# Window attention and SwiGLU on one core: block 0's down projections ahead of the third block's gates, and two groups of transposes moved from the matrix engine to the DMA crossbar

## The chip, the cores and the metric

The kernel runs on one core of a Trainium2 chip. The core has a matrix engine (PE, with its weight loads shown as PEld), a vector engine (DVE), an activation engine (ACT), a general engine (POOL) and a sync engine (SP). Each takes its instructions in order and waits at semaphores. SP, ACT and POOL also issue DMA transfers, which 16 DMA engines carry out. The metric is device time in microseconds (us) from launch to end, as the median over runs.

## The reference

Two stages. First attention with a window of 128 positions and 4 sink positions (the first four keys, which every query sees), for 4 batches, 8 heads, 768 positions, head size 64. Then a SwiGLU layer over the 3072 tokens, width 512, hidden width 1536.

```python
def _attn_ref(q, k, v, n_sink, window):
    scores = scale * np.matmul(q, k.transpose(0, 1, 3, 2))
    keep = is_sink | in_window                     # pos < 4, or 0 <= rel < 128
    scores = np.where(keep, scores, -1000000000.0)
    a = np.exp(scores - np.max(scores, axis=-1, keepdims=True))
    a = a / (np.sum(a, axis=-1, keepdims=True) + 1e-09)
    return np.matmul(a, v).astype(np.float32)

def _moe_ref(x, w_gate, w_val, w_out):
    g = x @ w_gate
    silu = g * (1.0 / (1.0 + np.exp(-g)))
    return (silu * (x @ w_val) @ w_out).astype(np.float32)
```

The output of the attention, heads side by side, is x of the second stage.

## The kernel before

**Groups and blocks.** The attention runs over 12 groups of 256 queries (three per batch), the second stage over blocks of tokens: 256, 256, 256, 512, 512, 512, 512, 256. Blocks 0 and 1 (groups 0 and 1) share their gate matmuls ("01"), the third block, number 2, is group 2, and block 3 is groups 3 and 4.

**A group's steps.** load_nat fetches keys (i = 0) and queries (i = 1) of a group by POOL's DMA queue into a tile nat, in two halves of 128 rows each. They have to be turned so that the head dimension lies on partitions (tiles kT and qT). Either step_TN does it on PE (four 128x128 transposes for a half, tile pn, with an eviction by ACT or DVE, L283 or L285), or xbar does it by DMA transposes that SP issues (L293). step_S, or step_S1 to S3 from group 3 on, are the scores and their exponentials; step_K is the sinks' part (matmuls mm_K with kss, which step_ks fills, and an exponential). step_PV multiplies with the values and normalises into xn, on DVE, or on ACT where its last argument is "a". step_X turns xn into the second stage's operand xT: for groups in PEX on PE (tile px, L543, evicted at L546 or L550), for the others by a DMA transpose of SP (L538).

**Second stage.** A unit gate makes hidden slices: project with w_gate into pg (L564), a tanh on ACT (L584), project with w_val into pv, and two DVE operations (L592, and L598, L603 or L607) that write the slice into ht. A unit down makes 128 rows of output: 12 matmuls over ht and w_out (pd, L657), a copy to ot (L662), and an output DMA that ACT issues for blocks 0 to 2 and SP for the others (L665).

**Order.** Everything is written out by hand. A list us holds units (gates and downs), and weave runs them in turn; slots gives each unit, by its number, the attention steps that are put inside it. In the first weave the units 0 to 3 are the first gates of blocks 0 and 1, 4 to 11 their shared gates, 12 to 17 block 2's gates, 18 to 23 the downs of blocks 0, 1 and 2, two units each. Inside a gate the steps stand between the pg and the pv matmuls (a step marked ahead stands before pg), inside a down they are spread over its 12 matmuls. The DMA transposes of step_X, and some DVE work, are put into a list later, which flush empties at the end of a unit.

**Queues.** SP's DMA queue holds, in this order, early loads, eight small sink loads for group 0's batch, eight for the other batches (load_sinks into vcl, L211), and then the crossbar transposes. Each DMA of SP and ACT takes one of eight completion lanes (semaphores) in turn, and waits until the lane's previous DMA has landed. The sink loads into vcl wait for a POOL memset (L815) that stands behind load_nat(3) and load_v(3). POOL's queue holds the weights and the groups' inputs: gates, nat of group 2, values, w_out in four parts (load_out, L169), nat and values of group 3, then those of group 4 and so on. From group 4 on there is one nat buffer, so load_nat(5) waits for the transposes of group 4.

Of the kernel before, what the change touches and what calls it, by code (L numbers as in the profile page):

```python
# [14 lines left out]
def kernel(  # L15
# [26 lines left out]
    SIZES = [256, 256, 256, 512, 512, 512, 512, 256]  # L42
    assert sum(SIZES) == NTOK and NG == 12
    OFF = [sum(SIZES[:i]) for i in range(len(SIZES))]
    PEX = (0, 1, 2)
    QG = [g for g in range(4, NG) if g % GC]
    ONE = range(3, NG)

# [57 lines left out]
    def load_nat(g):  # L106
        b, c = divmod(g, GC)
        x = (natp if g > 3 else rowp).tile(
            [P, 2, 2, DM], BF16, tag="nat" if g > 3 else "rows", name="nat")
        for i, src in ((0, k), (1, q)):  # L110
            for j in range(2):
                t0 = c * 256 + j * P
                nc.gpsimd.dma_start(  # L113
                    x[:, i, j].rearrange("p (h d) -> p h d", d=D),
                    src[b, :, t0:t0 + P].rearrange("h p d -> p h d"))
        nats[g] = x
# [67 lines left out]
    one = const.tile([P, 1], FP32)  # L184
# [338 lines left out]
    def step_X(g, j, evict="v"):  # L523
# [6 lines left out]
        elif tb > 1 and off == 0:  # L530
            xTs[tb] = dense(xtp.tile([P, DMC * 512], BF16, tag="xT", name="xT"),
                            DMC, SIZES[tb])
            if tb == 3:
                for i in range(2):
                    xTs[tb, i] = xTs[tb][:, :, 256 * i:256 * (i + 1)]
        if g not in PEX:
            def sp():
                nc.sync.dma_start_transpose(xTs[tb][:, :, off:off + P], xns[g, j])  # L538
# [128 lines left out]
    def gates(tb):  # L667
        return [(gate, tb, f) for f in range(0, DFC, 512 // SIZES[tb])]

    def downs(tb):  # L670
        return [(down, tb, t) for t in range(SIZES[tb] // P)]

    def A(fn, *a):
        return lambda: fn(*a)

    def TN(g, evict="av"):
        return [A(step_TN, g, i, j, evict) for j in range(2) for i in range(2)]
# [4 lines left out]
    def S1(g, apart=False):  # L682
        f = A(step_S1, g, apart)
        f.ahead = True
        return f

    def one(at, g, apart=False):
        return [(at, [S1(g, apart), A(step_S2, g, apart)]), (at + 1, [A(step_S3, g)])]

    def ahead(f):  # L690
        g = lambda: f()
        g.ahead = True
        return g

    def PVs(g):
        return [A(step_PV, g, j, hh) for hh in range(2) for j in range(2)]

    def Xs(g):
        return [A(step_X, g, j) for j in range(2)]
# [104 lines left out]
    load_gate(2)  # L804
    step_vsb(0)
    load_nat(2)
    load_gate(3)
    load_v(2)
    load_gate(4)
    load_gate(5)  # L810
    for i in range(4):
        load_out(i)
    load_nat(3)
    load_v(3)
    nc.gpsimd.memset(vcl, 0.0)  # L815
# [27 lines left out]
    for f in masks1[:3]:  # L843
        f()

    g0, g1, g2 = gates(0), gates(1), gates(2)
    us = [(gate_held, *g0[0][1:]), (gate_first, *g0[1][1:]), g1[0], g1[1],
          *((gate, "01", f) for f in range(4, DFC)),
          *g2, *downs(0), *downs(1), *downs(2)]

    def L(*fs):
        def f():
            for x in fs:
                x()
        return f

    def NV(g):
        return L(A(load_nat, g), A(load_v, g))
# [1 line left out]
    weave(us, slots(  # L860
        (4, TN(2)[::2]), (5, TN(2)[1::2]), ((6, 7), Ss(2)), (6, [K(2)]),
        ((8, 8), PVs(2)[:2]), (9, [A(step_PV, 2, 0, 1, "a"), A(step_PV, 2, 1, 1, "a")]),
        ((10, 11), [A(step_X, 2, 0, "a"), ahead(A(step_X, 2, 1, "a"))]),
        (11, [NV(4), lambda: nc.gpsimd.tensor_copy(out=vcl[64:128], in_=vcl[0:64])]),
        ((14, 14, 15, 15), TN(3, "aa")),
        (15, [A(xbar, 4)]), (15, [A(load_nat, 5)]), (19, [A(xbar, 5, (0,))]),
        *one(17, 3), (18, [A(step_ks, 1)]), (18, [A(step_vsb, 1)]),
        ((19, 19, 19, 20), PVs(3)), (19, [S1(4)]), (20, [L(A(step_S2, 4), A(step_S3, 4))]), (20, Xs(3)), (20, [A(xbar, 5, (1,))]),
        ((21, 21, 21, 22), PVs(4)), (21, Xs(4)[:1]),
        (22, [Xs(4)[1], flush, A(behind, 3, 511), A(load_v, 5), A(load_nat, 6)]),  # L870
        (23, [A(xbar, 6), A(turned, 6), A(load_v, 6), NV(7)])))
# [53 lines left out]
```

## Time and profile before

Three runs: 233.52 us median, 232.6 to 233.66.

| What | Value |
|---|---|
| profiled execution, its own time | 233.03 us |
| its span, first to last instruction | 231.2 us |
| DVE, ACT, POOL busy | 151.1, 106.3, 84.8 us |
| pg and pv matmuls (L564), 736 | 74.2 + 74.1 us |
| pd matmuls (L657), 300 rows in the trace | 65.9 us |
| POOL's DMA queue (q0) | 79,904 packets, 14.29 MB, 80.7% of 16 engines' span |
| SP's DMA queue (q1) | 30,672 packets, 11.58 MB, 28.5% |

Busy times are unions of an engine's instructions over the span. A matmul row's duration includes its way through the pipeline, so the cost of a matmul in a row of them is read from the starts of neighbouring rows. A row "engine line <- releaser: total, times, longest" is idle time of the engine and what ended it. A queue's share is the time that its packets took; it can be high where packets wait for each other, and shares of several queues can add to over 100%.

### The profile page before, as it was taken

How to read it: one execution, taken by the hardware profiler on the slowest of the kernel's cores; microseconds unless marked ns; L12 is line 12 of the kernel's file. 1: busy time of each engine (PE TensorE's matmuls, PEld its weight loads, DVE VectorE, ACT ScalarE, POOL GpSimd, SP SyncE). 2: the span in 40 equal slices, each digit the busy share in tenths (PEclk: the TensorE clock that was granted, in tenths of full speed). 3: DMA queues.
4: the chain of work that ended last, by engine and by line, in shares of the span. 5: the costliest groups of instructions: out<-in, count | busy, mean ns of one | idle time of the engine just before them, and what ended most of it. 6: DMA issues, size and time to landing. Idle time of an engine off the chain costs nothing.

```text
span 231.2 us, 5467 instructions
## 1 busy us (share of the span) xinstructions
PE 226.0 (98%) x2171; PEld 126.8 (55%) x2171; DVE 151.1 (65%) x327; ACT 106.3 (46%) x212; POOL 84.8 (37%) x123
## 2 busy tenths in 40 slices
PE   7989999999999999999999999999999999999994
PEld 3669545786556854455454454454454544487443
DVE  5898888767650797960897960697960599778000
ACT  4784496367523827323626412735512823333221
POOL 8997965960500906904526064362000000000000
PEclk9999999999999999999999999999999999999999
DMA  7999999999998998998999999989814102000132
GB/s 134 164 188 178 179 199 206 163 155 125 154 168 211 80 132 103 145 197 124 134 124 118 147 87 203 144 107 131 94 48 136 48 0 45 3 0 0 69 116 91
DMA packets 112008, 28.04 MB, mean 121 GB/s; under 512 B 99056, under 2 KB 109040, under 8 KB 111984
## 3 DMA queue, kind: packets, MB, share of 16 engines
q0 software_dynamic: 79904, 14.29, 80.7%
q1 hardware_dynamic: 30672, 11.58, 28.5%
q10 hardware_dynamic: 1408, 1.84, 2.8%
q8 instruction: 17, 0.28, 0.5%
q14 instruction: 7, 0.06, 0.1%
HBM read 29.13 MB, written 6.29 MB: 153 GB/s over the span
## 4 chain that ended last, share of the span: by engine, by line
PE 93%; DMA 4%; DVE 1%; ACTq 0%; ACT 0%; issue 0%
PE pg L564 27%; PE pv L564 27%; PE pd L657 27%; PE o L494 3%; PE s L382 3%; DMA wg<-in_moe_w_gate_dram 3%; DMA st<-in_q_dram 2%; PE o L463 1%; PE pn L279 1%; PE o L454 1%; PE pk L432 1%; PE s L326 0%; PE px L543 0%; DVE kT L755 0%; PE pt L746 0%; PE s L765 0%
## 5 line engine op out<-in xcount | busy, mean ns | idle before, releaser
L592 DVE SCALAR_TENSOR_TENSOR u<-th,pg 128x512 bf16<-128x512 f32 x72 | 49.1, 683 | 45.3 <-ACT th L584 44.9
L564 PE MATMUL pg<-xT,wg 128*128 128x512 bf16 (+1 forms) x368 | 74.2, 333 | 0.5 <-DMA wg<-in_moe_w_gate_dram 0.5
L564 PE MATMUL pv<-xT,wv 128*128 128x512 bf16 (+1 forms) x368 | 74.1, 333 | 0.0
L584 ACT ACTIVATE th<-pg 128x512 f32<-128x512 f32 x72 | 43.8, 608 | 59.4 <-PE pg L564 59.2
L657 PE MATMUL pd<-wo,ht 128*128 128x512 bf16 (+2 forms) x300 | 65.9, 370 | 0.0
L564 PEld LDWEIGHTS <-wg 128*128 128x128 bf16 x368 | 35.2, 98 | 26.5 <-DMA wg<-in_moe_w_gate_dram 0.7
L564 PEld LDWEIGHTS <-wv 128*128 128x128 bf16 x368 | 34.6, 98 | 22.8 <-issue 0.2
L607 DVE TENSOR_TENSOR ht<-u,pv 128x512 bf16<-128x512 bf16 x60 | 41.2, 686 | 4.5 <-PE pv L564 0.4
L657 PEld LDWEIGHTS <-ht 128*128 128x128 bf16 x300 | 27.6, 98 | 28.4
L662 ACT ACTIVATE ot<-pd 128x512 f32<-128x512 f32 (+1 forms) x24 | 14.3, 595 | 50.2 <-PE pd L657 50.2
L395 ACT ACTIVATE e<-s 128x512 bf16<-128x512 f32 x54 | 28.5, 614 | 5.8 <-PE s L382 5.4
L113 POOL DMA_DIRECT2D nat<-in_k_dram x20 | 17.8, 896 | 28.6 <-DMA qT<-nat 27.1
L511 DVE TENSOR_TENSOR xn<-o,rcp 128x256 bf16<-128x256 f32 x45 | 17.9, 420 | 0.7
L128 POOL DMA_DIRECT2D vm<-in_v_dram x24 | 17.8, 772 | 1.1 <-DMA va<-in_v_dram 0.8
L113 POOL DMA_DIRECT2D nat<-in_q_dram x20 | 17.8, 908 | 1.0 <-DMA wg<-in_moe_w_gate_dram 0.8
L494 PEld LDWEIGHTS <-e 128*128 128x128 bf16 x256 | 11.5, 98 | 6.0 <-issue 0.2
L404 DVE TENSOR_TENSOR e<-e,maskq 128x768 bf16<-128x768 bf16 x24 | 13.1, 552 | 1.9 <-ACT e L395 1.9
L151 POOL DMA_DIRECT2D va<-in_v_dram x12 | 10.7, 921 | 4.5 <-DMA wo<-in_moe_w_out_dram 2.5
L703 POOL CAST warmed<-xT 1x1 f32<-1x1 bf16 x3 | 0.5, 175 | 28.5 <-DMA xT<-xn 28.5
L503 DVE RECIPROCAL rcp<-o 128x4 f32<-128x4 f32 x48 | 7.1, 171 | 4.8 <-PE o L494 4.5
L664 DVE TENSOR_SCALAR ot<-pd 128x128 f32<-128x128 f32 x1 | 0.3, 292 | 14.3 <-PE pd L657 14.3
L333 ACT ACTIVATE e<-s 128x512 bf16<-128x512 f32 x16 | 8.3, 625 | 0.3 <-PE s L326 0.3
(86 smaller groups left out, 141.4 us busy)
## 6 DMA issues: line engine op xcount, KB each, us to landing
out_dram<-ot SPq DMA_DIRECT2D x17, 256.0 KB
nat<-in_k_dram POOLq DMA_DIRECT2D x20, 128.0 KB, 4.2
nat<-in_q_dram POOLq DMA_DIRECT2D x20, 128.0 KB, 5.2
va<-in_v_dram POOLq DMA_DIRECT2D x12, 128.0 KB, 5.5
wg<-in_moe_w_gate_dram POOLq DMA_DIRECT2D x6, 256.0 KB, 7.1
wv<-in_moe_w_val_dram POOLq DMA_DIRECT2D x6, 256.0 KB, 7.6
wo<-in_moe_w_out_dram POOLq DMA_DIRECT2D x4, 384.0 KB, 11.1
out_dram<-ot ACTq DMA_DIRECT2D x6, 256.0 KB
```

What stands on the lines that cost most here:

```text
L113: nc.gpsimd.dma_start(x[:, i, j].rearrange("p (h d) -> p h d", d=D), src[b, :, t0:t0 + P].rearrange("h p d -> p h d"))
L128: nc.gpsimd.dma_start(vms[b][p0:p1, t - 1, :, 0:D], v[b, :, t0:t0 + p1 - p0].rearrange("h p d -> p h d"))
L395: nc.scalar.activation(e_t[g][:, e0:e0 + 512], pss[g][w, i], AF.Exp, scale=scale)
L404: nc.vector.tensor_tensor(e, e, m.broadcast_to([P, 2, 384]), op=ALU.mult)
L494: nc.tensor.matmul(o, l, r, start=(c == 0 and i == 0), stop=(i == len(mms) - 1), skip_group_check=True)
L511: nc.vector.tensor_tensor(xn, po[:, :, 0:D], rcp.broadcast_to([P, 4, D]), op=ALU.mult)
L564: nc.tensor.matmul(ps[:, i * n:(i + 1) * n], ws[fi][:, c, fo * P:(fo + 1) * P], xTs[tb][:, c], start=(c == 0), stop=(c == DMC - 1))
L584: nc.scalar.activation(th, pg, AF.Tanh, scale=0.5)
L592: nc.vector.scalar_tensor_tensor(u, th, 1.0, pg, op0=ALU.add, op1=ALU.mult)
L607: nc.vector.tensor_tensor(hts[tb][:, f:f + 512 // SIZES[tb]].rearrange("p a n -> p (a n)"), u, pv, op=ALU.mult)
L657: nc.tensor.matmul(po, hts[tb][:, f, ts * P:(ts + 1) * P], wos[f // n][:, f % n, lo:hi], start=(f == 0), stop=(f == DFC - 1))
L662: nc.scalar.activation(ot, po, AF.Copy, scale=0.5)
```

## The change

Three things. Block 0's two downs stand ahead of block 2's six gates, so that units 12 and 13 are downs and 14 to 19 block 2's gates. Group 2 leaves PEX, so its xn is turned by two DMA transposes of SP (put into unit 9, behind the PV steps) in place of PE and ACT. Group 3's queries are turned by two DMA transposes (unit 12), while its keys stay on PE (units 14 and 15); load_nat(3) fetches queries before keys. The steps of group 3 and the start of group 4 move with them: scores of group 3 from unit 17 to 16, PV(3) from the downs of block 0 into gates 18 and 19 with the second half normalised on ACT, step_ks(1) and step_vsb(1) from unit 18 to 20, scores of group 4 from units 19 and 20 to 20 alone.

```diff
-    PEX = (0, 1, 2)
+    PEX = (0, 1)
...
-        for i, src in ((0, k), (1, q)):
+        for i, src in (((1, q), (0, k)) if g == 3 else ((0, k), (1, q))):
...
-          *g2, *downs(0), *downs(1), *downs(2)]
+          *downs(0), *g2, *downs(1), *downs(2)]
...
-        ((10, 11), [A(step_X, 2, 0, "a"), ahead(A(step_X, 2, 1, "a"))]),
+        (9, [flush, *Xs(2)]),
         (11, [NV(4), lambda: nc.gpsimd.tensor_copy(out=vcl[64:128], in_=vcl[0:64])]),
-        ((14, 14, 15, 15), TN(3, "aa")),
+        (12, [A(xbar, 3, (1,))]), ((14, 15), [A(step_TN, 3, 0, j, "aa") for j in range(2)]),
         (15, [A(xbar, 4)]), (15, [A(load_nat, 5)]), (19, [A(xbar, 5, (0,))]),
-        *one(17, 3), (18, [A(step_ks, 1)]), (18, [A(step_vsb, 1)]),
-        ((19, 19, 19, 20), PVs(3)), (19, [S1(4)]), (20, [L(A(step_S2, 4), A(step_S3, 4))]), (20, Xs(3)), (20, [A(xbar, 5, (1,))]),
+        *one(16, 3), ((18, 18), PVs(3)[:2]),
+        (19, [A(step_PV, 3, 0, 1, "a"), A(step_PV, 3, 1, 1, "a")]),
+        (20, [L(A(step_ks, 1), A(step_vsb, 1)), S1(4), L(A(step_S2, 4), A(step_S3, 4))]),
+        (20, Xs(3)), (20, [A(xbar, 5, (1,))]),
```

In the built programs this takes 16 transposes off PE, and puts four DMA transposes on SP's queue, two of xn into xT and two of nat into qT, right behind the eight sink loads into vcl and ahead of group 4's transposes. The transposes of xn have the lanes of the first two of those sink loads, the transposes of nat the next two. ACT's two output DMAs of block 0 have the lanes of the first and of the fourth of the new transposes.

## The prediction

> **What bounds the kernel now.** I read the page's busy shares first, then the chain of waits, then what the matrix engine waited for after the opening.
>
> ```profile
> span 231.2 us, 5467 instructions
> PE 226.0 (98%) x2171; PEld 126.8 (55%) x2171; DVE 151.1 (65%) x327; ACT 106.3 (46%) x212; POOL 84.8 (37%) x123
> DMA  7999999999998998998999999989814102000132
> PE 93%; DMA 4%; DVE 1%; ACTq 0%; ACT 0%; issue 0%
> PE pg L564 <- DMA wg<-in_moe_w_gate_dram: 0.5, 1, 0.5
> ```
>
> PE is the bound: 98% busy, 93% of the chain, and in the last line (PE's waits from 15 us to the end) one wait of 0.5 us. So PE work taken away is time won, and any PE wait put in is time lost, to the end. The DMA row matters as much: all 16 engines are full for two thirds of the span, and this change puts four transfers into the fullest stretch and makes PE wait for two of them.
>
> Next the timeline of PE, with start and length. The start of the next row gives the step.
>
> ```profile
> 38.84 0.39 PE L543 MATMUL px<-ident,xn 128*128 128x128 bf16 x4
> 39.06 1.03 PE L564 MATMUL pv<-xT,wv 128*128 128x512 bf16 x4
> ...
> 41.88 1.04 PE L564 MATMUL pg<-xT,wg 128*128 128x256 bf16 x8
> ...
> 46.24 0.61 PE L279 MATMUL pn<-ident,nat 128*128 128x128 bf16 x8
> 46.69 1.04 PE L564 MATMUL pv<-xT,wv 128*128 128x256 bf16 x8
> ...
> 67.78 5.13 PE L657 MATMUL pd<-wo,ht 128*128 128x512 bf16 x23
> 72.75 1.04 PE L564 MATMUL pg<-xT,wg 128*128 128x256 bf16 x8
> ```
>
> Four px transposes cost 0.22 us, eight pn transposes 0.45, a pd matmul (72.75 - 67.78) / 23 = 0.216.
>
> Last the queues: SP's timeline, SP's waits from 40 to 46 us, POOL's rows before them, and ACT around one output.
>
> ```profile
> 40.65 2.67 SPq L211 DMA_DIRECT2D vcl<-in_v_dram  x8
> 49.52 2.58 SPq L293 DMA_TRANSPOSE kT<-nat  x2
> 52.20 2.52 SPq L293 DMA_TRANSPOSE qT<-nat  x2
> ...
> SPq L293 <- DMA vcl<-in_v_dram: 2.3, 1, 2.3
> ...
> 39.48 0.88 POOL L151 DMA_DIRECT2D va<-in_v_dram  x1 [1.47 <-DMA wo<-in_moe_w_out_dram]
> 40.35 0.28 POOL L815 MEMSET vcl<- 128x195 f32 x1
> ...
> 64.06 0.63 ACT L662 ACTIVATE ot<-pd 128x512 f32<-128x512 f32 x1
> 65.83 0.34 ACTq L665 DMA_DIRECT2D out_dram<-ot  x1
> ```
>
> SP's eight sink loads of L211 wait for POOL's memset at 40.35, which stands behind value loads that wait for room in POOL's queue. SP issues them until 43.3 and then waits 2.3 us more: the next entry, here the first transpose, needs the first sink load to have landed, which the trace's semaphore record puts at 45.62 (4.97 us for 3 KB, because POOL's queue is backed up). The last pair shows the same rule on ACT: the output was ready at 64.69 and issued at 65.83, just after the kT transpose issued at 61.98, whose completion lane it shares, landed (65.75).
>
> **The change, part by part.** *PE work removed.* The two px groups go (0.22 + 0.22), and half of each pn group (0.225 + 0.22): 0.88 us. Nothing is added on PE. This is the whole gain.
>
> *Block 0's downs moved.* 24 pd matmuls, 24 x 0.216 = 5.2 us, stand at slots 12 and 13. PE reaches them at 41.88 - 0.44 = 41.44 and the third block's first gate at 46.6. Their own inputs are there: the last wo quarter landed at 42.63 (semaphore record) and is needed at 41.44 + 9 x 0.216 = 43.4; the last ht slice was done at 43.39 at the latest and is needed at 43.8. Cost nothing; without that cover, under 1 us.
>
> *Group 2's output by the crossbar.* Its two transposes stand in SP's queue behind the eight sink loads, and the first waits for the same lane as the first transpose does now. So although xn is ready at about 39.5, they issue at 45.64 and, at 1.3 us each (2.58 / 2), 46.94. PE needs both landed at 46.6, when the second is not yet issued. How late? From the semaphore record, a transpose on a quiet queue lands 2.40 us after its issue (those of 172.36 and 193.34): 49.3 at the soonest. Six times in this trace four transposes follow each other while POOL's loads are in flight (first issues at 49.52, 94.96, 110.91, 123.22, 142.47, 155.65). The second of the four landed 6.24, 6.89, 7.32, 8.71, 7.65 and 7.18 us after the first issue, the fourth 7.20, 8.67, 8.17, 9.57, 9.02 and 9.47. Here twelve of POOL's loads land between 45.6 and 55.4 us, so I take the medians: second at 45.64 + 7.25 = 52.9, fourth at 45.64 + 8.85 = 54.5. PE waits 52.9 - 46.6 = 6.3 us (2.7 to 7.8). Behind that wait stands all of PE's work.
>
> *Group 3's queries by the crossbar.* They are transposes three and four. The second of downs(0)'s outputs has the same lane as the fourth (a wait in the changed program), so ACT stands at that output from about 47.5 until 54.5. Behind it are the next two tanhs and the two kT copies that S1(3) needs: 0.36 (issue) + 0.49 + 0.47 + 0.49 (steps from tanh to copy to tanh to copy in the rows at 46.45 to 49.13) + 0.58 and 0.15 for the hand-overs, so S1(3) at 57.1. Without waits it would start at 46.6 + 3.92 (four groups of 0.87, two of 0.22) = 50.5. By PE's own path it starts at 52.9 + 3.92 = 56.8. The two waits overlap almost wholly: 6.6 us together.
>
> *The clock after the wait.* No row shows PE after a long wait. The nearest is the opening.
>
> ```profile
> 1.19 3.17 PE L730 MATMUL w<-zero 128*128 128x512 bf16 x7 [1.19 <-DVE one L191]
> 4.28 1.47 PE L746 MATMUL pt<-ident,x 128*64 128x128 bf16 x16
> ```
>
> Seven 512-wide matmuls step by 0.427 us there, half the pace of 0.216, and those 3.0 us without a gap did not end it. Bounds: nothing, or all 3.92 us before S1(3) at half pace (+3.9). I take the 3.0 us: 1.5 us more, so S1(3) at 56.8 + 1.5 = 58.3, 7.8 us late. The profile's granted clock reads 1.0 even there, so steps must be read.
> [...]
>
> *At nothing.* Group 3's hh=1 norms on ACT: eight more small activations, 1.75 us as one group at 37.70, in a slot where ACT has slack. Without it, up to 1.75. Queries loaded ahead of keys: same bytes; keys land where queries did (45.47, 46.34) and are needed after 47. step_ks in slot 20 leaves DVE some 0.3 us before mm_K; at worst 0.5. xbar(4) issues behind four more transposes (5.2 us), group 5's loads on POOL wait for it, and group 3's X stands behind group 5's keys on SP; now that X lands at 69.97 for a gate at 72.91, and a PE that is 7 us late gives it more room, not less.
>
> *Sum.* -0.88 + 7.8 = +6.9. The profiled execution took 233.03 (span 231.2, 1.8 around it; the median is 233.52): 239.9 us.
>
> **Rivals.** [...] 16%.
> *The clock holds:* S1(3) at 57.1: 233.03 + 5.7 = 238.7. For: nothing but the lack of a row. 20%.
> *Deeper:* second transpose at 8.71 (54.35), then all work before S1(3) at half pace: 62.2, 11.7 late, 243.8. For: POOL's backlog here is the deepest of the kernel, and the opening stayed slow until 10.5 us, with gaps. 12%.
> *The cover suffices* (the other side): the sink loads land in time for the pair to be issued by 42.9, so that both land (1.3 + 2.4 later) at 46.6. Then PE never waits: 233.03 - 0.88 = 232.2. It decides at an issue 2.7 us sooner than the trace's 45.64; nothing before that point moves on POOL or SP, so I see no reason. 5%.
> *It does not do what it says:* the added order on SP cannot vanish, and the PE work does; no chance kept.
>
> **How the numbers follow.** The forecast 239.9 has 47%. From 236.0 to 242.3 holds it, the clock that holds, and the quiet queue; the deeper case and the cover lie outside. A measurement tells 0.5% (1.2 us) from no change: faster 5% (the cover), same 2% (a wait of one to two us, which would need an issue sooner by about as much), slower 93%.
>
> **What would show it.** SP: two xT transposes at about 45.6 and 46.9 behind vcl. PE: px gone, 24 pd from 41.4, then a gap of about 6 us before the first 256-wide pg, "<- DMA xT<-xn". Steps of 256-wide matmuls after the gap near 0.215 instead of 0.109 for some 3 us. ACT: the second output issued when qT lands, near 54.5. From S1(3) on, rows as before, about 7 us later. Wrong if PE's gap at 46.6 is under 1 us, if the pair issues before 44, or if the loss sits elsewhere, after 75 us.

## The result, and the profile after

The change makes the kernel slower: 244.07 us (six runs, 243.36 to 244.77) against 233.18 us before (six runs, 232.6 to 233.89), a ratio of 1.0467 with an interval of 1.0438 to 1.0496. The prediction had the direction and the mechanism, but 239.9 us is 4.2 us short, and its range ended at 242.3. The profiled execution took 244.77 us with a span of 243.0, so 11.74 us are to be found against the 233.03 of before. In two experiments below, one run of four was over 1.5% slower than the fastest and is left out of the median and the range.

First the page of the changed kernel: busy shares, the rows by slices of 6.1 us, and the chain of waits.

```profile
span 243.0 us, 5450 instructions
...
PE 227.6 (94%) x2155; PEld 127.2 (52%) x2155; DVE 149.8 (62%) x325; ACT 106.0 (44%) x216; POOL 84.2 (35%) x123
...
PE   8789999709999999999999999999999999999994
...
PEclk9999999965999999999999999999999999999998
...
PE 73%; DMA 13%; POOL 8%; ACT 2%; DVE 1%; issue 1%; SPq 1%; POOLq 0%
```

PE's row falls to 7 in the eighth slice and to 0 in the ninth (48.6 to 54.7 us), and the granted clock to 6 and 5 in the ninth and tenth. The chain ran almost wholly over PE before (93%); now 22% of it goes over DMA, POOL and their queues. Busy PE time is 227.6 against 226.0 although 16 matmuls are gone, because some of the rest ran at half pace (granted clock 0.50 from 50.61 to 60.85, below).

Next the waits that end PE's and ACT's idle time from 15 us to the end (total, times, longest).

```profile
ACT ot L662 <- DMA xT<-xn: 7.9, 1, 7.9
PE pg L564 <- DMA xT<-xn: 7.9, 1, 7.9
ACT th L584 <- PE pv L564: 5.4, 1, 5.4
```

One long wait of PE and two of ACT are new. The third is named after PE, but lies behind an output issue that waited, as ACT's timeline shows. PE's timeline puts the first in its place.

```profile
41.69 5.34 PE L657 MATMUL pd<-wo,ht 128*128 128x512 bf16 x24
54.91 1.86 PE L564 MATMUL pg<-xT,wg 128*128 128x256 bf16 x8 [7.88 <-DMA xT<-xn]
...
57.00 1.91 PE L564 MATMUL pv<-xT,wv 128*128 128x256 bf16 x8
58.71 1.91 PE L564 MATMUL pg<-xT,wg 128*128 128x256 bf16 x8
...
61.82 0.84 PE L382 MATMUL s<-qT,kT 64*128 64x256 bf16 x18
...
71.06 1.02 PE L382 MATMUL s<-qT,kT 64*64 64x192 bf16 x35
72.34 0.45 PE L382 MATMUL s<-qT,kT 64*64 64x128 bf16 x17 [0.26 <-DVE ht L607]
72.72 0.29 PE L432 MATMUL pk<-qT,kss 128*32 128x128 bf16 x8
...
75.78 0.29 PE L454 MATMUL o<-vsb,es 32*128 32x260 bf16 x4 [0.29 <-ACT es L438]
...
84.26 1.04 PE L564 MATMUL pg<-xT,wg 128*128 128x256 bf16 x8
```

Read by starts of rows, the stretch up to block 3's first gate (72.75 before, 84.26 now: 11.51 later) adds up. The downs start 0.25 later than the 41.44 that the prediction works out, a drift of the opening. Their last matmul is reached at 41.69 + 24 x 0.215 = 46.85, and PE stands until 54.91: 8.06. Units 14 and 15 then take 61.82 - 54.91 = 6.91 in place of 3.92: 3.0 for half pace (eight 256-wide matmuls take 58.71 - 57.00 = 1.71, and took 0.87 before). From there to 84.26 pass 22.44. Before, downs and gates together took 72.75 - 41.88 = 30.87; less 0.445 for the transposes that are gone, 5.16 for the downs and 3.92 for the two units, 21.35 is left for the same work: 1.1 more now. All the missing transposes give 0.88 back: 0.25 + 8.06 + 3.0 + 1.1 - 0.88 = 11.5. The last 0.3 us come after 84.26.

The 1.1 us are to be seen at group 4's scores: from 71.06 to mm_K at 72.72 pass 1.66, where before (59.45 to 60.28, below) it was 0.83, and the sinks' exponential adds a wait of 0.29.

```profile
59.45 0.89 PE L382 MATMUL s<-qT,kT 64*64 64x192 bf16 x52
60.28 0.30 PE L432 MATMUL pk<-qT,kss 128*32 128x128 bf16 x8
```

DVE's timeline in the changed kernel says what stops these scores on their way.

```profile
70.83 0.66 DVE L592 SCALAR_TENSOR_TENSOR u<-th,pg 128x512 bf16<-128x512 f32 x1
71.59 0.69 DVE L607 TENSOR_TENSOR ht<-u,pv 128x512 bf16<-128x512 bf16 x1
```

These are DVE's two operations on the last slice of block 2, which end at 71.49 and 72.28. The semaphores show two stops: the scores go on at 71.55, released by the first, and at 72.34, released by the second. The scores read neither result; the kernel takes pg, pv and the scores from one pool of eight buffers (psum, L76), and these operations are the last readers of pg and pv.

SP's queue, and ACT's rows around block 0's two outputs.

```profile
40.81 2.66 SPq L211 DMA_DIRECT2D vcl<-in_v_dram  x8
45.92 2.62 SPq L538 DMA_TRANSPOSE xT<-xn  x2
48.63 2.68 SPq L293 DMA_TRANSPOSE qT<-nat  x2
```

```profile
44.48 0.60 ACT L662 ACTIVATE ot<-pd 128x512 f32<-128x512 f32 x1 [2.80 <-PE pd L657]
52.57 0.36 ACTq L665 DMA_DIRECT2D out_dram<-ot  x1
52.98 0.60 ACT L662 ACTIVATE ot<-pd 128x512 f32<-128x512 f32 x1 [7.90 <-DMA xT<-xn]
58.52 0.36 ACTq L665 DMA_DIRECT2D out_dram<-ot  x1
58.99 0.60 ACT L584 ACTIVATE th<-pg 128x512 f32<-128x512 f32 x1 [5.41 <-PE pv L564]
59.48 0.58 ACT L283 COPY kT<-pn 128x512 bf16<-128x512 bf16 x1
60.65 0.60 ACT L584 ACTIVATE th<-pg 128x512 f32<-128x512 f32 x1 [0.59 <-PE pg L564]
61.15 0.58 ACT L283 COPY kT<-pn 128x512 bf16<-128x512 bf16 x1
```

SP issues the pair for xT at 45.92 and 47.34, right after the first sink load has landed (45.84 by the trace's semaphore record). That record has the four transposes landing at 52.49, 54.78, 56.03 and 58.45, so 6.58, 7.43, 7.40 and 8.47 us after each one's own issue. ACT finished its first output copy at 45.08, issued it at 52.57, just after the first xT transpose landed, and issued the second at 58.52, just after the second query transpose landed. Only then come the tanh and the kT copies that S1(3) needs. So two things end almost together, at 61.7 and 61.8 us: the kT copies that ACT's hold has delayed, and PE's slow units.

The clock is best read in windows cut at its changes (columns: window, length, busy time of PE, PEld, DVE, ACT, POOL, granted clock, DMA share, GB/s; the share counts the whole time of the packets that start in a window, so it can pass 1).

```profile
46.85:50.61 3.76, 0.18 (x1) 0.00 (x0) 0.00 (x0) 0.00 (x0) 3.13 (x4) 1.00 2.37 155
50.61:54.91 4.30, 0.00 (x0) 0.03 (x1) 0.00 (x0) 0.60 (x1) 0.34 (x1) 0.50 1.82 149
54.91:60.85 5.94, 5.94 (x33) 4.35 (x34) 1.13 (x2) 1.27 (x3) 0.00 (x0) 0.50 1.75 183
60.85:61.82 0.97, 0.97 (x10) 0.69 (x10) 0.78 (x2) 0.88 (x2) 0.00 (x0) 1.00 0.06 6
```

The clock halves 3.76 us after the last matmul and is back 5.94 us after PE goes on, 10.24 us in all. At half pace 5.94 us hold 2.97 us of work, which is the loss of 3.0 found above.

### The profile page after: what moved, and what is told of

Its sections match the earlier page's. It is cut to its first block, busy times and chain, and to the rows that moved or that the text cites. A ratio compares the mean times of both kernels' runs of the same rounds, so it can differ in the third digit from the quotient of the medians.

```text
span 243.0 us, 5450 instructions
## 1 busy us (share of the span) xinstructions
PE 227.6 (94%) x2155; PEld 127.2 (52%) x2155; DVE 149.8 (62%) x325; ACT 106.0 (44%) x216; POOL 84.2 (35%) x123
## 4 chain that ended last, share of the span: by engine, by line
PE 73%; DMA 13%; POOL 8%; ACT 2%; DVE 1%; issue 1%; SPq 1%; POOLq 0%
PE pd L657 22%; PE pg L564 22%; PE pv L564 21%; DMA wo<-in_moe_w_out_dram 4%; DMA wv<-in_moe_w_val_dram 3%; DMA xT<-xn 3%; PE s L382 3%; PE o L494 2%; DMA vcl<-in_v_dram 2%; POOL va L151 2%; POOL nat L113 1%; ACT e L395 1%; POOL rows L102 1%; POOL wv L162 1%; PE o L463 1%
## 5 line engine op out<-in xcount | busy, mean ns | idle before, releaser
L564 PE MATMUL pg<-xT,wg 128*128 128x512 bf16 (+1 forms) x368 | 75.9, 339 | 8.5 <-DMA xT<-xn 7.9
L564 PE MATMUL pv<-xT,wv 128*128 128x512 bf16 (+1 forms) x368 | 75.0, 336 | 0.0
L564 PEld LDWEIGHTS <-wg 128*128 128x128 bf16 x368 | 35.9, 100 | 35.7 <-issue 8.8
L395 ACT ACTIVATE e<-s 128x512 bf16<-128x512 f32 x54 | 28.4, 621 | 2.9 <-PE s L382 2.9
L511 DVE TENSOR_TENSOR xn<-o,rcp 128x256 bf16<-128x256 f32 x43 | 16.9, 419 | 0.6
L494 PEld LDWEIGHTS <-e 128*128 128x128 bf16 x256 | 11.3, 98 | 5.2 <-issue 0.3
L382 PE MATMUL s<-qT,kT 64*64 64x64 bf16 (+4 forms) x366 | 8.4, 218 | 0.3 <-DVE ht L607 0.3
```

What stands on the lines that cost most here:

```text
L382: nc.tensor.matmul(pss[g][w, lo // 8][part, 64 * (lo % 8):64 * (lo % 8) + 64 * (hi - lo)], kTs[b][r, p, k0:k0 + kn], qTs[b][r, p, cc:cc + ...
L395: nc.scalar.activation(e_t[g][:, e0:e0 + 512], pss[g][w, i], AF.Exp, scale=scale)
L494: nc.tensor.matmul(o, l, r, start=(c == 0 and i == 0), stop=(i == len(mms) - 1), skip_group_check=True)
L511: nc.vector.tensor_tensor(xn, po[:, :, 0:D], rcp.broadcast_to([P, 4, D]), op=ALU.mult)
L564: nc.tensor.matmul(ps[:, i * n:(i + 1) * n], ws[fi][:, c, fo * P:(fo + 1) * P], xTs[tb][:, c], start=(c == 0), stop=(c == DMC - 1))
```

## The experiments

Times are medians; ratios are to the kernel before, run beside it. Edits are made to the changed kernel unless said otherwise. The theory: PE waits for group 2's transposes, ACT for group 3's; both land late because they stand behind the sink loads and beside POOL's loads, and each wait hides the other. The rivals: only one of the pairs costs, the half clock costs, or the moved units and steps do.

**One pair at a time.** First group 2's xn back on PE, with group 3's queries left on the crossbar.

```diff
-    PEX = (0, 1)
+    PEX = (0, 1, 2)
...
-        (9, [flush, *Xs(2)]),
+        ((10, 11), [A(step_X, 2, 0, "a"), ahead(A(step_X, 2, 1, "a"))]),
```

> The changed kernel with group 2's output turned by PE again (units 10 and 11, as before); downs, queries and the rest stay changed. Theory (PE waits at the third block's first gate for the crossbar's two xT transposes, 8 us, and comes back at half pace, 3 us): that gap is gone; the queries' pair now stands first on SP, issues at 45.9 and 47.2 and is needed by S1(3) at about 51, so a smaller wait of 0 to 4 us may stand there: 233 to 237.5 us. Rival (the queries' pair, which holds ACT through a shared completion lane, is what costs): still 241 or more.

Measured 243.2 us, ratio 1.0421 (1.0391 to 1.0451): almost nothing is won, which is the rival's case. PE's timeline of this run:

```profile
57.21 0.39 PE L382 MATMUL s<-qT,kT 64*128 64x256 bf16 x2 [5.25 <-ACT kT L283]
...
59.37 1.89 PE L564 MATMUL pg<-xT,wg 128*128 128x256 bf16 x8
```

The wait at the gate is gone, and another stands two units later. The query transposes are now first in SP's queue, land at 52.94 and 55.54, and ACT issues block 0's outputs at 53.01 and 55.62, so that kT is copied late. The pace is half again from 54.99 to 61.81. Then the other way round, group 3's queries back on PE and group 2's xn on the crossbar.

```diff
-        (12, [A(xbar, 3, (1,))]), ((14, 15), [A(step_TN, 3, 0, j, "aa") for j in range(2)]),
+        ((14, 14, 15, 15), TN(3, "aa")),
```

> The changed kernel with group 3's queries turned by PE again (units 14 and 15); group 2's output stays on the crossbar. Theory: the gap before the third block's first gate stays at about 8 us (first pg at 54 to 55) with half pace behind it; only what ACT adds goes: 242 to 244.5. Rival (queries' pair and its lane): 236 or less.

Measured 244.39 us, 1.0491 (1.0451 to 1.0531). PE waits 7.79 us for xT, and S1(3) starts at 61.22.

```profile
54.56 1.86 PE L564 MATMUL pg<-xT,wg 128*128 128x256 bf16 x8 [7.79 <-DMA xT<-xn]
...
61.22 0.84 PE L382 MATMUL s<-qT,kT 64*128 64x256 bf16 x18 [0.33 <-ACT qT L283]
```

Either pair alone costs nearly as much as both. So both edits together, the two diffs above:

> The changed kernel with group 2's output and group 3's queries both turned by PE again; block 0's downs stay ahead, and the steps of groups 3 and 4 where the change put them. Theory (the whole loss is in the crossbar transposes, which land 7 to 9 us after issue, and either pair alone costs nearly all of it): PE does not wait at the third block's gates nor at S1(3); 233.0 to 234.8, with 1.4 us of small waits around S1(4) as its upper part. Rival (the moved downs and steps cost by themselves): 236 or more.

Measured 235.56 us, 1.0092 (1.0065 to 1.0119). This lies between the two expectations. It is the reorder with its moved steps, without the crossbar, and it costs 2.2 us; the crossbar pairs cost the other 8.5 (244.07 - 235.56), the PE work that they save already taken off. PE's timeline here:

```profile
52.90 0.84 PE L382 MATMUL s<-qT,kT 64*128 64x256 bf16 x18 [1.18 <-ACT qT L283]
...
62.14 0.99 PE L382 MATMUL s<-qT,kT 64*64 64x192 bf16 x35
63.40 0.45 PE L382 MATMUL s<-qT,kT 64*64 64x128 bf16 x17 [0.26 <-DVE ht L607]
```

Block 3's first gate starts at 75.32, 2.57 later than before: 0.1 from the opening, 1.3 before S1(3), because ACT's first output, copied by 45.39, is issued only at 48.31, when the sink load on its lane has landed (48.23), and 1.1 at S1(4), as in the changed kernel.

**The sink loads out of the way.** vcl is cleared by DVE at the start and its loads are issued right behind group 0's, so that nothing small stands ahead of the transposes.

```diff
+    nc.vector.memset(vcl, 0.0)
+    nc.vector.memset(vcl[:, :, D:D + 1], 1.0)
...
     load_sinks(vcf, 0, 1)
+    load_sinks(vcl, 1, B)
...
-    nc.gpsimd.memset(vcl, 0.0)
-    nc.gpsimd.memset(vcl[:, :, D:D + 1], 1.0)
-    load_sinks(vcl, 1, B)
```

> The changed kernel with the eight sink loads into vcl issued on SP right behind the first eight, at 5 to 9 us (their memset on DVE), so that SP's queue is free when xn is ready at 39.7. Theory (issue time sets the landing): xT pair issues at about 39.8 and 41.1, lands 5 to 7.5 us later, 46 to 48.5; PE's gap is 0 to 2 us, the clock stays full: 233.5 to 236.5. Rival (the backlog of POOL's queue sets the landing whenever the pair is issued): lands near 53 to 55 as before, 242 to 244.

Measured 241.92 us, 1.034 (1.0284 to 1.0397): the pair lands as the theory has it, the time is close to the rival's. The pair goes out at 39.39 and 40.78 and still takes 7.08 and 7.38 us, but that is early enough (lines are 3 higher here):

```profile
48.30 1.03 PE L567 MATMUL pg<-xT,wg 128*128 128x256 bf16 x8 [0.79 <-DMA xT<-xn]
...
57.19 0.40 PE L385 MATMUL s<-qT,kT 64*128 64x256 bf16 x2 [4.80 <-ACT kT L286]
```

The gate's wait falls from 7.88 to 0.79, and the time by only 2 us: the queries land at 51.95 and 55.52, ACT's second output leaves at 55.60, and S1(3) waits 4.80 for the copy behind it. To take ACT out of it as well, block 0's outputs go to SP, on top of the edit above.

```diff
-            (nc.scalar if tb < 3 else nc.sync).dma_start(out[r0:r0 + P, lo:hi], ot)
+            (nc.scalar if 0 < tb < 3 else nc.sync).dma_start(out[r0:r0 + P, lo:hi], ot)
```

> The kernel with the sink loads early, and block 0's two output transfers issued by SP, so that ACT has no wait for a completion lane. Theory (ACT, held at an output until the queries' second transpose lands, delays the kT copies): tanh and copies are done by 53, S1(3) starts when the queries land, near 55.5 instead of 57.2 and 58.2; 238.5 to 240.5 against 241.9. Rival (the landing alone decides): 241.5 to 242.

Measured 236.91 us (236.29 to 237.61), 1.0153 (1.0117 to 1.0189), better than expected. The transposes take as long (7.5 to 7.8 us each), yet PE waits only for what they bring:

```profile
49.12 1.03 PE L567 MATMUL pg<-xT,wg 128*128 128x256 bf16 x8 [1.24 <-DMA xT<-xn]
...
54.55 0.84 PE L385 MATMUL s<-qT,kT 64*128 64x256 bf16 x18 [1.33 <-DMA qT<-nat]
```

Two waits of 1.2 to 1.3 us, and a clock that stays whole here. So ACT's hold, which no instruction of the attention asks for, cost 5 us (241.92 - 236.91), the half pace behind its wait of 4.80 us (0.5 from 55.87 to 62.70 in the run above) included.

**The half clock.** 32 matmuls of zeros, 512 wide, stand ahead of unit 14; their result is used by nothing.

```diff
+        (14, [ahead(lambda: fill(32, bank([P, 512], FP32, "w"), 512))]),
```

> The changed kernel with 32 matmuls of zeros, 512 wide (32 x 0.216 = 6.9 us), on PE between block 0's downs and the third block's first gate, inside the wait. They compute nothing that is used. Theory (the half pace after the wait comes from PE's idleness): 256-wide steps after the wait are 0.109 in place of 0.21, 3 us won: 240.5 to 241.7. Rival (half pace has another cause, such as contention with the transfers): 244 as before.

Measured 243.91 us, 1.0468 (1.0428 to 1.0507), no gain. The granted clock is 1.0 until the end of the span, and both units that were slow run at full pace:

```profile
56.29 1.03 PE L564 MATMUL pg<-xT,wg 128*128 128x256 bf16 x8 [2.13 <-DMA xT<-xn]
...
60.32 0.28 PE L382 MATMUL s<-qT,kT 64*128 64x256 bf16 x2
61.09 0.73 PE L382 MATMUL s<-qT,kT 64*128 64x128 bf16 x16 [0.49 <-ACT kT L283]
```

ACT's second output leaves at 58.52, to the hundredth as in the changed kernel, and S1(3) cannot go on before its kT copies (the row at 61.09). Half pace cost 3.0 us on PE, in time that PE would mostly have spent waiting for ACT: the row after these scores starts at 61.75, against 62.59 in the changed kernel, and the profiled executions differ by 0.85 us (243.92 and 244.77), the medians by 0.16. That xT landed 1.4 us later in this execution (56.15) was hidden in the same way. The same filling where ACT does not wait for query transposes, that is with the queries on PE as in the second experiment:

```diff
-        (12, [A(xbar, 3, (1,))]), ((14, 15), [A(step_TN, 3, 0, j, "aa") for j in range(2)]),
+        (14, [ahead(lambda: fill(32, bank([P, 512], FP32, "w"), 512))]),
+        ((14, 14, 15, 15), TN(3, "aa")),
```

> The kernel with the queries on PE (244.4: PE waits 7.8 us for xT and goes on at half pace), with 32 matmuls of zeros in the wait, which compute nothing that is used. Here no queries' transposes hold S1(3) behind it. Theory (the half pace costs 1.5 to 3 us where nothing else binds): 241.5 to 243.0. Rival (the half pace is hidden anyway, as it was with the changed kernel's zeros): 244 to 244.8.

Measured 243.41 us, 1.0418 (1.0366 to 1.047), 1.0 us below the 244.39 without filling, though the two intervals overlap. S1(3) starts at 60.35 in place of 61.22, in line with it.

**What stretches the transposes.** POOL's loads of group 4 (queries, keys, values) are held until group 3's queries have been turned.

```diff
-        (11, [NV(4), lambda: nc.gpsimd.tensor_copy(out=vcl[64:128], in_=vcl[0:64])]),
+        (11, [lambda: nc.gpsimd.tensor_copy(out=vcl[64:128], in_=vcl[0:64])]),
+        (13, [flush, A(turned, 3), NV(4)]),
```

> The changed kernel with POOL's loads of group 4 (keys, queries, values) held until the second transpose of group 3's queries has landed; nothing else moves. Theory (POOL's loads in flight stretch the transposes): the pair of xT still issues at 45.9 and 47.2 but lands by 50.5, the queries by 52.5; PE's gap falls from 8 to about 3.5 us, S1(3) starts near 55: 237 to 240. Rival (the transposes are slow by themselves at this place): 243 to 245.

Measured 242.2 us (240.25 to 243.61), 1.0373 (1.031 to 1.0436), between the two expectations. The pairs are issued as before (46.23, 47.63, 48.92, 50.44) and land after 2.90, 3.88, 3.14 and 2.59 us, in place of 6.6 to 8.5. That settles what stretches them here: group 4's loads in flight. How the loads do it is not shown. The time follows only by 1.9 us, and PE's timeline says why:

```profile
51.64 1.87 PE L564 MATMUL pg<-xT,wg 128*128 128x256 bf16 x8 [3.95 <-DMA xT<-xn]
...
58.49 0.84 PE L382 MATMUL s<-qT,kT 64*128 64x256 bf16 x18
```

The wait is halved, but 3.95 us are still enough for the clock to fall (0.5 from 50.64 to 57.47), and S1(3) starts at 58.49. All three cures together, sink loads early, outputs by SP and POOL's loads held:

> The changed kernel with all three: sink loads early, block 0's outputs issued by SP, group 4's loads held until group 3's queries are turned. Theory: xT pair issued at 39.4 and 40.8, landed by 47.5, queries by 49.5, no long wait at the third block's gates or S1(3); S1(4) may wait a microsecond for group 4's own transposes: 233.5 to 236.5. If the loss had another root than these three: above 238.

Measured 240.86 us (238.42 to 241.58), 1.0297 (1.0228 to 1.0365), far over the 233.5 to 236.5 expected. S1(3) now starts at 52.62 without a wait, and the loss has moved on:

```profile
52.62 0.86 PE L385 MATMUL s<-qT,kT 64*128 64x256 bf16 x18
...
66.34 0.89 PE L385 MATMUL s<-qT,kT 64*64 64x192 bf16 x52 [4.39 <-DMA qT<-nat]
```

Group 4's loads were the backlog. Held back, they make group 4's queries land at 65.79 and 66.20, S1(4) waits 4.39 us, and the clock halves again (67.24 to 70.65).

**Is there a version that beats the kernel before?** The reorder with all turning on PE, sink loads early and outputs by SP:

> The kernel with both pairs on PE (235.6), and in addition the sink loads early and block 0's outputs issued by SP. Theory (of its 2.2 us over the kernel before, 1.2 come from ACT, held at the two outputs by lanes of the sink loads, so that the kT and qT copies and S1(3) are late, and 1.4 from small waits around S1(4)): the wait at S1(3) goes, S1(4)'s stay: 234.1 to 234.8. Rival (the moved steps alone cost it): 235.4 or more.

Measured 234.91 us (12 runs), 1.0057 (1.0035 to 1.0079), just over the expected range. The wait at S1(3) falls from 1.18 to 0.33 us; the 1.1 us at S1(4) stay.

```profile
51.92 0.84 PE L385 MATMUL s<-qT,kT 64*128 64x256 bf16 x18 [0.33 <-ACT qT L286]
```

To reach the 1.1 us, S1(4) stands two matmuls later in the down, and group 3's second norms go back to DVE, on top of this.

```diff
-        (19, [A(step_PV, 3, 0, 1, "a"), A(step_PV, 3, 1, 1, "a")]),
-        (20, [L(A(step_ks, 1), A(step_vsb, 1)), S1(4), L(A(step_S2, 4), A(step_S3, 4))]),
+        (19, PVs(3)[2:]),
+        (20, [L(A(step_ks, 1), A(step_vsb, 1)), L(), L(), S1(4), L(A(step_S2, 4), A(step_S3, 4))]),
```

> The same as with ACT freed and both pairs on PE, and S1(4) two matmuls later in its down, group 3's second norms on DVE as before the change. Theory (the small waits around S1(4) come from DVE and ACT being behind after unit 19): 0.5 to 1.2 us less than that kernel, 233.2 to 234.0. Rival (they come from PSUM banks alone): no difference.

Measured 235.15 us (12 runs), 1.0072 (1.0047 to 1.0097): no gain. The scores at 63.82 are one row now, with no idle time named, but still take 1.61 us until mm_K:

```profile
63.82 1.47 PE L385 MATMUL s<-qT,kT 64*64 64x192 bf16 x52
65.43 0.29 PE L435 MATMUL pk<-qT,kss 128*32 128x128 bf16 x8
```

From S1(3) to block 3's first gate pass 22.21 us (54.15 to 76.36), in place of 22.41 in the run above: 0.2 us won, in a profiled execution whose opening was 2.2 us late. The semaphores say that DVE still holds S1(4), by other work: the scores go on at 64.51 and 64.84, released by the last slice's ht (done at 64.45) and by the first of the two norms brought back to DVE (64.79), and mm_K by the copy of step_ks behind them (65.37). So the later place was used up by the norms. That S1(4) would be free if it stood further behind block 2's last gate is an argument, and no run shows it. Last, this kernel with group 3's queries on the crossbar, the one part of the change that looked cheap once ACT was free.

```diff
-        ((14, 14, 15, 15), TN(3, "aa")),
+        (12, [A(xbar, 3, (1,))]), ((14, 15), [A(step_TN, 3, 0, j, "aa") for j in range(2)]),
```

> That last kernel with group 3's queries on the crossbar again, now first on SP, to issue when they are loaded, near 44.7 and 46.0. Theory (7 to 7.5 us under POOL's loads): landed by 52.5 to 53.5, S1(3) needed at 51.9, so 0.44 us of PE saved against a wait of 0 to 1.5: 233.2 to 235. A version that beats the kernel before would have to come out under 232.8.

Measured 238.03 us (236.19 to 239.02), 1.0175 (1.013 to 1.022), against 233.2 to 235 expected, and 2.9 us worse than with the queries on PE. They go out at 44.23 and 45.61, land after 7.90 and 8.50 us, and PE waits for them:

```profile
54.24 0.84 PE L385 MATMUL s<-qT,kT 64*128 64x256 bf16 x18 [1.70 <-DMA qT<-nat]
```

No version beat the kernel before.

## Why the prediction was right in direction and too small

**What held.** "This is the whole gain", 0.88 us: 16 matmuls are gone, and nothing more was won. "Cost nothing", of the downs: 24 matmuls without a wait from 41.69. The pair "issue at 45.64 and, at 1.3 us each (2.58 / 2), 46.94": 45.92 and 47.34, behind the sink loads, by the lane rule as read from the profile of before. In both traces the DMAs of SP and ACT use eight semaphores in turn, none goes out before the one ahead of it on its semaphore has landed, and a held one follows within 0.02 to 0.08 us: the output at 65.83 after 65.75 before, and here 45.92 after 45.84, 52.57 after 52.49 and 58.52 after 58.45. The releaser "<- DMA xT<-xn", the ACT hold at the second output, and "The two waits overlap almost wholly" are all in the trace, and the last is what the experiments on single parts ran into. The rivals fell: the transposes landed 6.6 to 8.5 us after their issue and not 2.40, the clock did not hold (0.5 for 10.24 us), and the cover did not suffice. The 16% of the quiet queue, and with them the range's lower end of 236.0, took a wait of PE until 49.3, 2.7 us, to cost nothing of the clock. No run shows that term: a wait of 2.13 us left the granted clock at 1.0 (with filling ahead of it), and one of 3.95 was followed by 0.5 (with POOL's loads held). What came is the deeper case, 243.8 us, which had 12% and stood outside the range: it put S1(3) 11.7 us late, and 11.3 were measured; like the forecast it had nothing for S1(4). One reading was loose: what the prediction calls "room in POOL's queue" is the lane rule again, with eight lanes of POOL's own. In the trace of before each of POOL's loads from 28.18 to 37.14 goes out 0.28 to 0.29 us after the load eight places ahead of it has landed.

**The landing term was too small.** The step was "I take the medians: second at 45.64 + 7.25 = 52.9, fourth at 45.64 + 8.85 = 54.5". Measured from the first issue, the second took 8.86 us and the fourth 12.53. Of the wait's 8.06 us, 6.3 were forecast: 1.8 short. Even the worst of the six groups of before, 8.71 and 9.57, was short, so they were no fair sample. The run with POOL's loads held shows that these loads set the landing (2.6 to 3.9 us without them), and in the changed kernel POOL issued nine of them for group 4 from 42.39 to 49.69, around this pair; the value loads among them landed up to 60.09. The prediction counted them ("twelve of POOL's loads land between 45.6 and 55.4 us") and then took the median over six other places.

**The clock term was half of what it became.** The step was "I take the 3.0 us: 1.5 us more". The half pace lasted 5.94 us of work and took 3.0. In the six runs whose clock fell in a wait or just behind one, 3.70 to 5.94 us passed from PE's going on until it was back. The term's 3.0 us, read from the opening for lack of a row behind a long wait, were shorter than any of these. But this term did not decide: with the pace kept up by filling, the time was 243.91. ACT's outputs held S1(3) until 61.09 anyway.

**ACT's hold was mis-sized with the landing.** "ACT stands at that output from about 47.5 until 54.5" became 58.52, after a first stand from 45.08 to 52.57 at the first output, and S1(3) behind ACT became about 61 in place of 57.1. So the "7.8 us late" at S1(3) is 11.3 (61.82 against 50.5).

**A part costed "at nothing" cost 1.1 us.** The moved steps of groups 3 and 4 double the time of S1(4), 0.83 to 1.66 us, and add 0.29 at the sinks. The forecast for this part allowed 0.5 us at worst and sought it in step_ks on DVE. It was DVE, but with block 2's last slice, right behind which the change puts S1(4). With 0.25 of drift at the opening and 0.3 after 84.26, the terms give 6.9 + 1.8 + 1.5 + 1.1 + 0.25 + 0.3 = 11.85, against 11.74 in the profile.

**What the sum could not say.** Three hindrances stand at one place: xT for the gate, the queries with ACT's copies for S1(3), the pace between them. As their ends coincide near 61 us, each of them alone costs nearly everything, and taking one away wins 0.2 us (filling), 0.9 (xT by PE), 2.2 (sink loads early) or nothing (queries by PE). Both pairs taken off the crossbar win 8.5.

## What to carry to other kernels

A transfer that an engine must wait for is costed by its place in its queue and by what other queues have in flight at that moment, and not from the median of other places: here even the worst of them was short, 9.57 us for the fourth transpose where 12.53 were measured, and with POOL's loads held the same transposes took 2.6 to 3.9 us in place of 6.6 to 8.5. When two engines share completion lanes in turn, as SP and ACT do here (the second output went out at 58.52, behind a transpose of its lane that landed at 58.45), look up whose transfer an output issue will wait for, and what is queued behind that issue on its engine: giving block 0's outputs to SP was worth 5 us with the sink loads early. An experiment that undoes one of several hindrances at the same place shows only the next, so undo them in pairs before calling one harmless.

## What the runs showed of the hardware

**Transposes and POOL's loads.** A DMA transpose of 128x512 bf16 landed 2.40 to 2.45 us after its issue on a quiet queue (the four from 172.36 on in the trace of before). With POOL's loads in flight the fours of the six groups in that trace took 2.9 to 7.0 us each, the two pairs of the changed kernel 6.6 to 8.5, and one 9.2 with the sink loads early. With group 4's loads held back the same pairs took 2.6 to 3.9. With all three cures the pair for xT, issued at 39.31 and 40.71 while POOL's earlier loads were landing, took 7.14 and 7.74, so it need not be group 4's loads.

**The clock after a wait.** In the six profiled executions whose granted clock fell in a wait of PE or just behind one, it stood at 0.5 for 10.24 us in the changed kernel, 6.83 with one pair, with sinks early and with loads held, and 3.41 with all three cures: three times, twice and once 3.41. A wait of 3.95 us (loads held) was enough and one of 2.13 (behind the filling) was not. The clock fell 3.76 us after PE's last matmul in the changed kernel and 2.95 with the loads held (50.64, PE until 47.69). With all three cures it fell at 67.24, when PE had been going on for 0.9 us (from 66.34) after its wait of 4.39. It was back 3.70 us after PE went on in the second experiment and 5.94 in the changed kernel. What sets these times is not shown.

**Filling kept the clock.** 32 matmuls on zeros, 7.07 us, in stretches of 9.2 us (47.08 to 56.29) and 8.2 us (47.23 to 55.47) held the granted clock at 1.0 there in the two profiled executions that had them: the eight 256-wide matmuls behind the wait took 0.87 us in both, and 1.66 in the changed kernel.
